# V of batches 2 and 3 issued by GpSimd, piece by piece, in place of SyncE

## The chip, the cores and the metric

The kernel runs on one core of one Trainium2 chip. The metric is device time in microseconds (us) of one execution. The engines of a core have short names in the profile: PE is TensorE (matmul), PEld its weight load, DVE is VectorE, ACT is ScalarE, POOL is GpSimd, SP is SyncE, which here only issues transfers. A transfer issued by POOL goes through one queue (q0, "software_dynamic"), one issued by SP through another (q1, "hardware_dynamic"); both are served by the same 16 DMA engines. Each engine works through its own instructions strictly in order, and waits on semaphores for the others.

## The reference

Eight batches of eight heads of causal attention with a learned decay, and behind them a gated feed-forward block. Shapes: q, k, v are 8 x 8 x 576 x 64, s is 8 x 8 x 576, the weights are 512 x 1536 (twice) and 1536 x 512, all float32.

```python
def _attn_ref(q, k, v, s):
    scores = scale * np.matmul(q, k.transpose(0, 1, 3, 2))
    causal = np.triu(np.ones((S, S), dtype=bool), k=1)
    cum = np.cumsum(np.maximum(s, 0.0), axis=-1)
    bias = -(cum[:, :, :, None] - cum[:, :, None, :])
    scores = np.where(causal, -1000000000.0, scores + np.minimum(bias, 0.0))
...
    return np.matmul(attn, v)

def _moe_ref(x, w_gate, w_val, w_out):
    g = x @ w_gate
    silu = g * (1.0 / (1.0 + np.exp(-g)))
    return (silu * (x @ w_val)) @ w_out
```

attn is the softmax of the scores, and x is the attention's output with the heads of a token side by side: 4608 tokens of 512.

## The kernel before, in words

**Units of work.** The attention goes head by head (64 of them, numbered 0 to 63, eight to a batch; the code calls the number `bh` or `kk`). Four heads are a head block (`hb`, or `h` in `side`, 16 of them; `HB = 4`, so two blocks to a batch); `step` is the head within its block. A head's scores are computed in four pieces, `ci` 0 to 3 (`score_piece`, L352): PE makes the products (L374), ACT the exponential into the tile `pt` (L384), and POOL puts zeros above the diagonal, for piece 0 at L387 and for piece 3, the tail of 64 columns, at L392. These two are "the masks". The product with V (`av_piece`, L409) comes one or more heads later, then DVE divides by the row sums (L425, L426).

**The feed-forward block** works on tiles of 512 tokens (`tt`). For each tile there are twelve gate blocks and twelve value blocks (L649, weights `wg` and `wv`), with ACT's tanh at L670 and DVE's products at L672 and L683, and then the product with w_out (L706 for the first two tiles, L755 for the later ones, which use a seven-product scheme). The weights are loaded by POOL, in halves or quarters (`w_load`, L346).

**How the two are woven.** PE's order is written out by hand. The head of the program (to about 40 us) computes the attention of batch 0 and begins the first token tile. Then a loop runs through the feed-forward items of each tile and, after each item, lets the generator `attn_items` go on to a position that grows with the items done (`pump`). After every score piece `attn_items` calls `side(h, step, ci)` and `side_v(h, step, ci)`, which issue what has its place there: loads, casts, copies. So a place such as (4, 2, 2) means: after score piece 2 of head 4 * 4 + 2 = 18. An entry such as (H + 4, 3), with H = 8, means: after score piece 3 of head 12. Some more loads are hung on items of the first tile (`at_item`).

**V.** `load_v` (L156) loads V of one batch in five pieces by token rows (four of 128 rows, 256 KB each, one of 64 rows), each one transfer, into the float32 tile `rawv`, of which there is one buffer. `cast_v` (L167) casts a piece to bfloat16 into `vt` (two buffers). V of batch 0 and 1 is loaded by POOL. V of batch 1 is cast by POOL at heads 11 and 12 (`V1_AT`). V of batch 2 is loaded by SP, with one call after score piece 3 of head 12 (L485), and cast by POOL at heads 17 and 18 (`V2_AT`, L540). V of batch 3 is loaded by SP, two pieces after head 18's piece 1 (L526), three after head 19's (L530), and cast by ACT at heads 21 to 23 (`V_AT`, L542, the cast itself is L171). V of batches 4 to 7 is loaded by SP and cast by ACT in the same way.

**K and Q.** `load_one` (L145) loads K or Q of one head block (576 KB) into one of three buffers each (`rawk`, `rawq`). Blocks 2 to 5 are loaded by POOL, blocks 6 and later by SP: block 6 after head 16's piece 1 (L487), block 7 after head 18's. They are cast to bfloat16 (`cast_one`, L258 on ACT, L260 on POOL). Up to block 4 PE transposes them (L301) and ACT or DVE copies them out (L328, L330). From block 5 on SP writes the cast to DRAM (`scratch`, L274), reads it back transposed (`transposes`, L284), and DVE copies the halves into the tile `kq` (`split`, L288). The rows of `kq` that carry the decay are copied from the tile `HL` by `aug` (L188), four small transfers for each block, issued by POOL from block 4 on.

**The rest of POOL's work** in the stretch of the change: the casts of K and Q of blocks 4 and 5, stores of finished outputs (L727), and from batch 2 on the writes of the attention's output to DRAM (`x_out`, L443), which SP reads back transposed (L450). Later POOL also makes subtractions for the feed-forward block (L692, L820).

Of the kernel before, what the change touches and what calls it, by code (L numbers as in the profile page):

```python
# [19 lines left out]
def kernel(  # L20
# [11 lines left out]
    nc = tc.nc  # L32
    PSUM = bass.MemoryType.PSUM

    B, H, S, D = q.shape
# [78 lines left out]
    with tc.manual_schedule():  # L114
# [26 lines left out]
        def load_one(hb, name, rs=(0, NR), eng=nc.sync):  # L141
            b, g = divmod(hb, 2)
            if rs[0] == 0:
                loaded[name, hb] = raw.tile([128, NR, J, D], FP32, tag="raw" + name, name="raw" + name)
            eng.dma_start(  # L145
                loaded[name, hb][:, rs[0] : rs[1], :, :].rearrange("x r j d -> x r (j d)"),
                SRC[name][0][b, g * HB + 2 * rs[0] : g * HB + 2 * rs[1], :, :].rearrange(
                    "(r e) (p j) d -> (e p) r (j d)", e=2, j=J
                ),
            )  # L150

        def load_qk(hb):
            load_one(hb, "k")
            load_one(hb, "q")

        def load_v(b, cs, eng=nc.sync):  # L156
            if 0 in cs:
                loaded["v", b] = raw.tile([128, NCH, H, D], FP32, tag="rawv", bufs=1, name="rawv")
            t = loaded["v", b]
            for c in cs:  # L160
                n = 128 if c < 4 else TAIL
                eng.dma_start(  # L162
                    t[0:n, c, :, :],
                    v[b, :, c * 128 : c * 128 + n, :].rearrange("h p d -> p h d"),
                )

        def cast_v(b, c, eng):  # L167
            n = 128 if c < 4 else TAIL
            dst, src_t = VT[b % 2][0:n, c, :, 0:D], loaded["v", b][0:n, c, :, :]
            if eng is nc.scalar:  # L170
                nc.scalar.copy(dst, src_t)  # L171
            else:
                eng.tensor_copy(dst, src_t)
# [9 lines left out]
        def aug(hb, engs, hhs=range(HB)):  # L183
            for hh in hhs:
                r, e = divmod(hh, 2)
                r0 = 64 * (1 - r)
                bh = hb * HB + hh
                engs[hh].dma_start(  # L188
                    KQ[hb % 2][r][r0 : r0 + 4, :, e * S : (e + 1) * S],
                    HL[bh : bh + 1, :, :, :],  # L190
                )
# [61 lines left out]
        def cast_one(hb, name, eng):  # L253
            cts[name, hb] = cp.tile([128, J, NR, D], BF16, tag="c" + name, bufs=2, name="c" + name)
            dst = cts[name, hb].rearrange("x j r d -> x r j d")
            src_t = loaded[name, hb]
            if eng is nc.scalar:
                nc.scalar.copy(dst, src_t)  # L258
            else:
                eng.tensor_copy(dst, src_t)  # L260
# [11 lines left out]
        def scratch(hb):  # L272
            for name, SC in (("k", KS), ("q", QS)):
                nc.sync.dma_start(  # L274
                    SC[hb].rearrange("(x j) c -> x (j c)", j=J),
                    cts[name, hb].rearrange("x j r d -> x (j r d)"),
                )
# [3 lines left out]
        def transposes(hb):  # L281
            for name, SC in (("k", KS), ("q", QS)):
                prs[name, hb] = cp.tile([128, NR * S], BF16, tag="p" + name, bufs=1, name="p" + name)
                nc.sync.dma_start_transpose(prs[name, hb], SC[hb])  # L284
# [185 lines left out]
        def do_later(n):  # L470
            while n > 0 and later:
                f, *args = later.pop(0)
                f(*args)
                n -= 1
# [2 lines left out]
            (H + 3, 3): (0, 1), (H + 4, 0): (2,), (H + 4, 1): (3,), (H + 4, 2): (4,)  # L477
        }

        def side(h, step, ci):  # L480
            bh = HB * h + step
            for c in V1_AT.get((bh, ci), ()):
                cast_v(1, c, nc.gpsimd)
            if bh == H + 4 and ci == 3:
                load_v(2, range(5))  # L485
            if h == 4 and (step, ci) in ((0, 1), (2, 1)):
                load_qk(6 + step // 2)  # L487
            if h >= 5 and h + 3 < NHB and (step, ci) == (0, 1):
                if h == 6:
                    load_one(h + 3, "k")  # L490
                else:
                    load_qk(h + 3)
            hb = h + 1
            if NPE <= hb < NHB:
                late = hb == NPE
                if late and (step, ci) == (0, 1):
                    scratch(hb)
                if late and (step, ci) == (0, 3):
                    transposes(hb)
                if (step, ci) == (0, 1):  # L500
                    aug(hb, GP4)
                first = 1 if hb < NPE + 3 else 0
                if step in (first, first + 1) and ci == (3 if late else 1):
                    for r in range(NR):
                        later.append((split, hb, "kq"[step - first], r))
            hb = h + 2
            if hb == NPE and step == 3 and ci % 2 == 1:
                cast_one(hb, "kq"[ci // 2], nc.gpsimd)
            if NPE < hb < NHB:
                six = hb == NPE + 1  # L510
                if (step, ci) == ((2, 0) if six else (0, 2)):
                    cast_one(hb, "k", nc.scalar)
                if (step, ci) == ((2, 2) if six else (1, 2)):
                    cast_one(hb, "q", nc.scalar)
                if (step, ci) == ((3, 0) if six else (2, 0)):
                    scratch(hb)
                if (step, ci) == (3, 3 if six else 0):
                    do_later(NR * 2)
                    transposes(hb)
            if ci != 1:  # L520
                return
            bn = h // 2 + 1
            if 3 <= bn < B:
                if h % 2 == 0:
                    if step == 2 and h != 6:
                        load_v(bn, (0, 1))  # L526
                    if step == 3:
                        if h == 6:
                            load_one(h + 3, "q")
                        load_v(bn, (2, 3, 4))  # L530
# [36 lines left out]
        def attn_items():  # L567
            for kk in range(H, BH + 2):
                h, step = divmod(kk, HB)
                if kk < BH:  # L570
                    if step == 0:
                        do_later(NR * 2)
                    if step == 1 and 3 < h + 1 < NPE:
                        cast_one(h + 1, "k", nc.gpsimd)
                        cast_one(h + 1, "q", nc.gpsimd)
                    if step == 2 and 3 < h + 1 < NPE:
                        aug(h + 1, GP4)
                    for ci in range(4):
                        score_piece(kk, ci)
                        side(h, step, ci)  # L580
                        side_v(h, step, ci)
                        yield kk + 0.1 + ci / 8
                        if (step, ci) in PREP_AT.get(h, ()):
                            prep_one(
                                h + 1, PREP_AT[h][step, ci],
                                (nc.scalar, nc.vector)[ci // 2] if h == 2 else None,
                            )
                            yield kk + 0.1 + ci / 8
# [327 lines left out]
        def pick(side):  # L916
            b = PICK[side]
            for lo in range(2):
                for c0, c1 in ((0, 512), (512, S)):
                    nc.tensor.matmul(  # L920
                        banks[:, b + c0 // 512, 0 : c1 - c0], sel[:, lo, :],
                        HL[:, lo, 1, c0:c1], start=(lo == 0), stop=(lo == 1),
                        skip_group_check=True,
                    )

        def picked_row(side):
            b = PICK[side]
            src_t = banks.rearrange("p b n -> p (b n)")[up, b * 512 : b * 512 + S]
            dst = KQ[0][0][up, side, 0:S]
            if side == 1:  # L930
                nc.scalar.activation(
                    dst, src_t, AF.Identity, bias=r_m[up, 0:1], scale=r_k[up, 0:1]
                )
            else:
                nc.vector.tensor_scalar(
                    dst, src_t, r_q[up, :], r_k[up, :], ALU.mult, ALU.add
                )
            give(b)
            give(b + 1)
# [195 lines left out]
```

## Time and profile before

| | |
|---|---|
| three runs, us | 372.74, 372.95, 375.08; median 372.95 |
| profiled execution, us | 372.82 (span of the profile 371.1) |
| granted TensorE clock | 1.0 |
| DMA, whole span | 64.21 MB, mean 173 GB/s |
| queue of SP (q1) | 79188 packets, 37.92 MB |
| queue of POOL (q0) | 13072 packets, 25.75 MB |
| V pieces issued by SP | 30, median 762 ns each (367 to 3786) |
| V pieces issued by POOL | 10, median 903 ns each (696 to 1322); 4.5 to 11.2 us from issue to landing, median 7.5 |

The whole span in 40 slices of 9.3 us each; a digit is the busy share in tenths:

```profile
PE   7899999999999999999999999999999999999995
DVE  8878786288985999589968987699768867975984
ACT  8979776778886976687858875786466423323321
POOL 8998785945366556694749465955575506315220
DMA  7999999999999975995699575996161113002003
```

A span is the time from the first to the last instruction of the profiled execution; the device time is a little longer. Times inside the profile are counted from the start of the span. In an order of time, a line gives start, length, engine, source line, operation, what is written and read, how many instructions were merged, and in brackets the idle time before and what ended it. A line of waits gives the engine and line that waited, for whom, the total, how many times, and the longest. "To landing" is the time from the issue of a transfer to its completion.

### The profile page before, as it was taken

How to read it: one execution, taken by the hardware profiler on the slowest of the kernel's cores; microseconds unless marked ns; L12 is line 12 of the kernel's file. 1: busy time of each engine (PE TensorE's matmuls, PEld its weight loads, DVE VectorE, ACT ScalarE, POOL GpSimd, SP SyncE). 2: the span in 40 equal slices, each digit the busy share in tenths (PEclk: the TensorE clock that was granted, in tenths of full speed). 3: DMA queues.
4: the chain of work that ended last, by engine and by line, in shares of the span. 5: the costliest groups of instructions: out<-in, count | busy, mean ns of one | idle time of the engine just before them, and what ended most of it. 6: DMA issues, size and time to landing. Idle time of an engine off the chain costs nothing.

```text
span 371.1 us, 8778 instructions
## 1 busy us (share of the span) xinstructions
PE 362.7 (98%) x3286; PEld 229.9 (62%) x3286; DVE 289.9 (78%) x583; ACT 241.2 (65%) x472; POOL 220.6 (59%) x336
## 2 busy tenths in 40 slices
PE   7899999999999999999999999999999999999995
PEld 6685566555555557755685568555865585476464
DVE  8878786288985999589968987699768867975984
ACT  8979776778886976687858875786466423323321
POOL 8998785945366556694749465955575506315220
PEclk9999999999999999999999999999999999999999
DMA  7999999999999975995699575996161113002003
GB/s 236 213 271 285 196 295 253 246 360 180 246 223 249 287 162 167 220 328 158 175 184 261 168 197 173 234 160 160 40 147 36 35 35 113 0 2 103 13 0 113
DMA packets 92301, 64.21 MB, mean 173 GB/s; under 512 B 72620, under 2 KB 78116, under 8 KB 92260
## 3 DMA queue, kind: packets, MB, share of 16 engines
q1 hardware_dynamic: 79188, 37.92, 44.1%
q0 software_dynamic: 13072, 25.75, 26.5%
q8 instruction: 25, 0.41, 0.5%
q14 instruction: 16, 0.13, 0.1%
HBM read 37.90 MB, written 19.86 MB: 156 GB/s over the span
## 4 chain that ended last, share of the span: by engine, by line
PE 88%; DVE 4%; POOL 4%; ACT 1%; issue 1%; DVEq 0%; POOLq 0%
PE banks L649 46%; PE banks L755 17%; PE banks L374 10%; PE banks L409 8%; PE banks L706 5%; DVE kq L330 2%; POOL rawv L162 1%; DVE pp L672 1%; DVE ht L683 1%; PE banks L301 1%; ACT pt L384 1%; PE banks L458 1%; DVE kq L288 0%; POOL ck L260 0%; POOL cq L260 0%
## 5 line engine op out<-in xcount | busy, mean ns | idle before, releaser
L384 ACT ACTIVATE pt<-banks 128x512 bf16<-128x512 f32 (+1 forms) x256 | 120.6, 511 | 28.2 <-PE banks L374 16.1
L649 PE MATMUL banks<-XT,wg 128*128 128x512 bf16 x432 | 111.4, 380 | 0.0
L649 PE MATMUL banks<-XT,wv 128*128 128x512 bf16 x432 | 110.9, 379 | 0.1
L670 ACT ACTIVATE th<-banks 128x512 bf16<-128x512 f32 x108 | 64.7, 599 | 54.8 <-PE banks L649 49.5
L672 DVE SCALAR_TENSOR_TENSOR pp<-th,banks 128x512 bf16<-128x512 bf16 x108 | 73.7, 682 | 19.4 <-ACT th L670 18.8
L683 DVE SCALAR_TENSOR_TENSOR ht<-pp,banks 128x512 bf16<-128x512 bf16 x108 | 74.1, 686 | 10.6 <-DVE pp L672 0.5
L374 PE MATMUL banks<-kq 128*128 128x128 bf16 (+4 forms) x576 | 76.3, 240 | 0.4 <-DVE kq L288 0.3
L692 POOL TENSOR_TENSOR ht<-ht 128x512 bf16<-128x512 bf16 x35 | 40.4, 1154 | 53.0 <-DVE su L690 52.9
L374 PEld LDWEIGHTS <-kq 128*128 128x128 bf16 x576 | 45.9, 98 | 29.8 <-issue 1.7
L649 PEld LDWEIGHTS <-wv 128*128 128x128 bf16 x432 | 38.4, 98 | 36.1 <-issue 0.2
L649 PEld LDWEIGHTS <-wg 128*128 128x128 bf16 x432 | 38.3, 98 | 33.6
L387 POOL TENSOR_SCALAR_AFFINE_SELECT pt<-pt 128x512 bf16<-128x512 bf16 x58 | 38.2, 658 | 24.8 <-ACT pt L384 22.7
L409 PEld LDWEIGHTS <-pt 128*128 128x128 bf16 x960 | 41.9, 98 | 17.4 <-issue 0.2
L409 PE MATMUL banks<-vt,pt 128*128 128x65 bf16 x960 | 46.8, 194 | 0.0
L443 POOL DMA_DIRECT2D xs<-ot x24 | 21.7, 903 | 29.3 <-DVE ot L426 28.7
L755 PEld LDWEIGHTS <-ht 128*128 128x128 bf16 x336 | 31.2, 98 | 4.3
L426 DVE TENSOR_TENSOR ot<-banks,rc 128x320 bf16<-128x320 f32 x64 | 31.5, 492 | 2.2
L188 POOL DMA_DIRECT2D kq<-HL x48 | 28.9, 604 | 0.5 <-issue 0.4
L706 PE MATMUL banks<-wo,ht 128*128 128x512 bf16 x96 | 25.8, 380 | 0.0
L755 PEld LDWEIGHTS <-su 128*128 128x128 bf16 x252 | 23.5, 98 | 3.3
L820 POOL TENSOR_TENSOR ysb<-ysb 128x512 f32<-128x512 f32 x12 | 15.2, 1270 | 15.3 <-DVE ysb L814 15.3
L755 PE MATMUL banks<-WS,ht 128*128 128x256 bf16 x168 | 22.9, 273 | 0.0
(101 smaller groups left out, 383.9 us busy)
## 6 DMA issues: line engine op xcount, KB each, us to landing
out_dram<-ysb POOLq DMA_DIRECT2D x32, 256.0 KB, 4.0
rawv<-in_v_dram SPq DMA_DIRECT2D x24, 256.0 KB
rawk<-in_k_dram SPq DMA_DIRECT2D x10, 576.0 KB
rawq<-in_q_dram SPq DMA_DIRECT2D x10, 576.0 KB
xs<-ot POOLq DMA_DIRECT2D x24, 160.0 KB, 3.5
ks<-ck SPq DMA_DIRECT2D x11, 288.0 KB
qs<-cq SPq DMA_DIRECT2D x11, 288.0 KB
rawk<-in_k_dram POOLq DMA_DIRECT2D x5, 576.0 KB, 7.5
```

The costliest lines, as they stand in the source:

```text
L374: nc.tensor.matmul(sc[:, o : o + w], T[:, 1, e * S + 128 * tj : e * S + 128 * (tj + 1)], T[:, 0, e * S + lo : e * S + hi], start=not maske ...
L384: nc.scalar.activation(pt[:, c0 : c0 + n], sc, AF.Exp, scale=0.125)
L387: nc.gpsimd.affine_select(pt[:, 1088:1600], pt[:, 1088:1600], pattern=[[0, 4], [1, 128]], compare_op=ALU.is_ge, fill=zreg, base=0, channel ...
L409: nc.tensor.matmul(av[:, bi * (D + 1) : (bi + 1) * (D + 1)], pt[:, c0 : c0 + 128], VT[b % 2][:, tj, h, :], start=(tj == 0), stop=(tj == bi),)
L426: nc.vector.tensor_mul(ot[:, :, e * D : (e + 1) * D], av3[:, :, 0:D], rc[:, :, None].to_broadcast([128, NCH, D]),)
L649: nc.tensor.matmul(view(bs, TT), w[:, c, f0 : f0 + 128], xt[:, c, :], start=(c == 0), stop=(c == 3),)
L670: nc.scalar.activation(th, pg, AF.Tanh, scale=0.5)
L672: nc.vector.scalar_tensor_tensor(pp, in0=th, scalar=1.0, in1=pg, op0=ALU.add, op1=ALU.mult)
L683: nc.vector.scalar_tensor_tensor(hp[:, 2 * k2 : 2 * k2 + 2, :].rearrange("p a n -> p (a n)"), in0=pp, scalar=0.5, in1=pv, op0=ALU.mult, op ...
L692: (nc.vector if ft == NFT - 1 else nc.gpsimd).tensor_sub(hp[:, 1:3, :], hp[:, 1:4:2, :], hp[:, 0:3:2, :])
L706: nc.tensor.matmul(view(pys[ts_], DM), hps[ft // 2][:, 2 * (ft % 2) + half, c0 : c0 + 128], WO[j][:, ft % WKO, :], start=(ft == 0), stop=( ...
L755: nc.tensor.matmul(ps, lhs(p), rhs(p), start=(first and p == 0), stop=(last and p == NP - 1), skip_group_check=True,)
```

## The change

The five pieces of V of batch 2 are no longer issued by SP in one call after head 12, but by POOL, one piece each after heads 12 (piece 3), 13 (pieces 1 and 3) and 14 (pieces 1 and 3). V of batch 3 is no longer issued by SP after heads 18 and 19, but by POOL, one piece each after head 18 (score piece 2), head 19 (pieces 0 and 2) and head 20 (pieces 0 and 2). The old calls are taken out: the condition `3 <= bn` becomes `3 < bn`, so that SP's calls remain for batch 4 and later. Within a place, the V load comes ahead of what `side` and `side_v` issue there after it.

```diff
+        V2_LOAD = {
+            (H + 4, 3): (0,), (H + 5, 1): (1,), (H + 5, 3): (2,), (H + 6, 1): (3,),
+            (H + 6, 3): (4,),
+        }
+        V3_LOAD = {
+            (4, 2, 2): (0,), (4, 3, 0): (1,), (4, 3, 2): (2,), (5, 0, 0): (3,), (5, 0, 2): (4,)
+        }
+
         def side(h, step, ci):
             bh = HB * h + step
             for c in V1_AT.get((bh, ci), ()):
                 cast_v(1, c, nc.gpsimd)
-            if bh == H + 4 and ci == 3:
-                load_v(2, range(5))
+            for c in V2_LOAD.get((bh, ci), ()):
+                load_v(2, (c,), nc.gpsimd)
+            for c in V3_LOAD.get((h, step, ci), ()):
+                load_v(3, (c,), nc.gpsimd)
             if h == 4 and (step, ci) in ((0, 1), (2, 1)):
                 load_qk(6 + step // 2)
...
             bn = h // 2 + 1
-            if 3 <= bn < B:
+            if 3 < bn < B:
                 if h % 2 == 0:
                     if step == 2 and h != 6:
                         load_v(bn, (0, 1))
```

## The prediction

> **What bounds the kernel now.** I read the page's first lines, then busy time by stage, then the longest waits of SP's queue, then the orders of time of SP, POOL, PE and DVE around the moved loads, and for single transfers the time from issue to landing.
>
> ```profile
> span 371.1 us, 8778 instructions
> PE 362.7 (98%) x3286; PEld 229.9 (62%) x3286; DVE 289.9 (78%) x583; ACT 241.2 (65%) x472; POOL 220.6 (59%) x336
> ```
>
> TensorE is the bound: it is idle for 8.4 us in all. The stages say where (columns: stage, length, busy time of PE, PEld, DVE, ACT, POOL, granted clock, DMA share, GB/s).
>
> ```profile
> 50.00:55.00 5.00, 5.00 (x67) 3.36 (x64) 4.11 (x9) 3.12 (x7) 4.99 (x8) 1.00 1.20 253
> 55.00:60.00 5.00, 5.00 (x71) 3.45 (x69) 3.44 (x8) 3.73 (x9) 3.66 (x8) 1.00 1.13 313
> 60.00:65.00 5.00, 5.00 (x70) 3.34 (x68) 3.56 (x8) 3.17 (x6) 1.88 (x4) 1.00 0.85 209
> ...
> 80.00:85.00 5.00, 4.75 (x42) 2.68 (x41) 4.87 (x11) 3.25 (x7) 3.26 (x6) 1.00 1.20 315
> ```
>
> V of batch 2 is loaded at 51 to 62 us, V of batch 3 at 76 to 83. In all of 40 to 100 us PE misses 0.26 us, at 82.42, before the scores of head 20, where it waits for a copy on DVE (L288). Nothing there waits for V. So the change has 0.26 us to win in its own stretch, and every new wait of PE is paid in full, for PE has no later gap to take it back.
>
> Next SP: its longest waits (us in total, times, longest), then its order of time (start, length).
>
> ```profile
> SPq L162 <- DMA rawv<-in_v_dram: 19.2, 2, 18.6
> SPq L162 <- POOL vt L173: 10.9, 2, 8.2
> ...
> 21.05 2.25 SPq L188 DMA_DIRECT2D kq<-HL  x2
> 50.98 10.69 SPq L162 DMA_DIRECT2D rawv<-in_v_dram  x5
> 61.71 0.62 SPq L145 DMA_DIRECT2D rawk<-in_k_dram  x1
> ```
>
> SP stands at the V load from 23.3 to 51.0: 18.6 us until V of batch 1 has landed, 8.2 more until POOL has cast it (there is one V buffer). Then it takes 10.7 us to issue five pieces. Behind them in SP's order is the load of K and Q of head block 6, at 61.71.
>
> **The change part by part.** *Removed from SP:* 10.69 us of issue, and 0.99 + 3.34 us for batch 3 at 75.97 and 79.71. By itself it gains nothing on PE; it shortens SP's road to the transposes of block 6, whose results DVE takes only at 90.7. I count 0.
>
> *Moved by it: K and Q of block 6.* Their three-deep buffers were last used by block 3, and POOL's casts of that block end at 36.88 + 1.16 = 38.04 (K) and 37.96 + 1.16 = 39.12 (Q). With the V load gone, nothing else holds SP, so these 1,152 KB are issued 23 us earlier. They meet these loads, which POOL put on its own queue and PE will want (last column: us to landing); below them, in order of time, who takes them:
>
> ```profile
> wv<-in_moe_w_val_dram POOLq DMA_DIRECT2D x1, 384.0 KB, 9.7
> rawk<-in_k_dram POOLq DMA_DIRECT2D x1, 576.0 KB, 10.5
> ...
> 47.91 1.03 PE L649 MATMUL banks<-XT,wv 128*128 128x512 bf16 x4
> 51.82 1.15 POOL L260 CAST ck<-rawk 128x1152 bf16<-128x1152 f32 x1
> 54.38 0.44 PE L301 MATMUL banks<-ident,ck 128*128 128x128 bf16 x5
> ```
>
> The last quarter of the value weights is issued at 36.11 and lands at 45.8; the tenth value block needs it at 47.91: 2.1 us of room. K of block 4, issued at 40.68, lands at 51.2 and is cast at 51.82. The 16 DMA engines are full there (share 1.1 to 1.3 in every stage from 24 to 60 us), so bytes put in push back what stands behind. How far: where the same two loads now run almost alone, at 64 to 68 us, the stage shows 386 GB/s, so 1.18 MB hold the engines for 3.1 us. Lower end 0 (they fit beside), upper end 6 us (the 190 GB/s of the full stages). I take 3.0, by the row of the very same loads. The weights then land at 48.8, and PE waits 48.8 - 47.91 = 0.9 us. K of block 4 lands at 54.2, is cast by about 55.35, and PE, already 0.9 late, wants it at 54.38 + 0.9 = 55.3: no second wait to speak of. **+0.9 us** (0 to 3.9, the end at 6 us of delay). The Trainium skill (DMA: Bandwidth & Descriptors, Queues, rings and completion order) says that each DMA engine goes round-robin between the queues that have work, a packet at a time, which is why a load from SP would not queue up behind POOL's. With that page's HBM limit of 358 GB/s the estimate would be 3.3 us of delay, a wait of 1.2, and 374.5 for the sum below.
>
> *Added to POOL: ten issues.* POOL's own V issues of batches 0 and 1 took 903 ns (median; 696 to 1322): 4.5 us for each batch (3.5 to 6.6). POOL's idle time is 0.01 + 1.34 + 3.12 = 4.5 us in 50 to 65, and 3.34 + 1.74 + 2.92 = 8.0 in 75 to 90, so both batches fit; what counts is what stands behind each piece in POOL's order. For batch 2: the casts of K and Q of block 4 (priced above), the masks of heads 13 to 15, and four small bias copies for block 4 (L188). They were issued from 56.01 on and the first landed 5.9 us later, at 61.9; the scores of head 16 need it at 65.69. With three pieces ahead (2.7 us) and casts that wait for late K and Q (1.5), the first goes out near 59.9 and lands at 65.8; PE wants it at 66.6. Cost 0, with 0.8 us to spare. The mask of head 14's tail, 59.90, moves to about 64 and is read near 66.5. The pieces need no new wait: POOL itself made the casts that free the buffer. Their data: V pieces from POOL landed in 7.5 us (at most 11.2), and the last one, issued near 64.5, is cast at 75.32.
>
> For batch 3 I follow POOL again, then DVE and PE (start, length; idle before in brackets):
>
> ```profile
> 77.91 0.23 POOL L392 TENSOR_SCALAR_AFFINE_SELECT pt<-pt 128x64 bf16<-128x64 bf16 x1 [1.48 <-ACT pt L384]
> 81.11 0.91 POOL L443 DMA_DIRECT2D xs<-ot  x1 [2.97 <-DVE ot L426]
> ...
> 76.52 0.45 DVE L288 COPY kq<-pk 64x1152 bf16<-64x1152 bf16 x1
> 81.33 0.95 DVE L288 COPY kq<-pq 64x1152 bf16<-64x1152 bf16 x1
> 82.42 0.38 PE L374 MATMUL banks<-kq 128*128 128x128 bf16 x4 [0.26 <-DVE kq L288]
> ```
>
> The first piece fits the 1.48 us gap at 76.43. Four more, 3.6 us, fall between 82.65 and 89.5; the mask of head 20's tail moves from 86.85 to about 89.5 and is read near 90.6. Cost 0, with 1 us to spare (with 1.32 us for each piece it would be 0.6 late). The casts of V on ACT, at 87.98 to 98.75, come 4 us or more behind the landings that 7.5 us would give for the first pieces, 2 us for the last.
>
> But the first piece lies upon the L288 copy at 76.52, and DVE works without a break from 75.12 to the copy that PE waits for. The same copy takes 0.45 us with POOL still and 0.95 at 81.33, with POOL issuing L443; at 142.29, under L188 issues, it took 0.45. So 0 to 0.9 us; I take the middle, which is also what the L443 row adds (0.95 - 0.45, less a little), an issue of 0.91 us like a V piece's: **+0.45 us**, and PE's wait at 82.42 grows from 0.26 to 0.7. The Trainium skill (SBUF — State Buffer, SBUF: two separate sides) has VectorE's two-port modes and GpSimd share a port pair as an exclusive lock, and its rules for kernel authors advise against issuing from GpSimd under such a copy. By a full lock the copy would wait out the whole 0.9 us issue, and the sum would be 374.6; the 0.45 at 142.29 speaks against a lock at every issue.
>
> **Sum.** The profiled execution took 372.82 us (span 371.1 and 1.72 around it), 0.13 below the median of the runs, 372.95. 372.82 + 0.9 + 0.45 = 374.2. That is the forecast.
>
> **Rivals.**
> *Nothing is late: not slower.* SP does run ahead, but the early K and Q delay the weights by less than their 2.1 us of room, and the copy at 76.52 keeps its 0.45 us. For it: the second half of w_out, issued at 45.58 with V of batch 2 coming in beside it, took 11.1 us to land, and the first half, issued at 39.25 with nothing beside it, 10.4; so a second queue need not cost its whole time. Against: the DMA share over 1, and V of batch 2 came in small packets, 10.7 us long, where K and Q come at once. Time 372.6 (the 0.26 us goes as well) to 373.1. It is also what comes of it if SP is held by something I don't see and issues block 6 no earlier, so that the change does not do what its order says. 30%.
> *The early loads hold POOL's queue back twice as long: slower by over 1%.* At the 190 GB/s end the delay is 6 us. The weights land at 51.8 and PE stands 3.9 us; K of block 4 lands at 57.2, is cast by 58.4, and PE, by then 3.9 late, comes for it at 58.3, so that wait isn't paid again; POOL's pieces and bias copies, behind the late casts, move by no more than PE. 372.82 + 3.9 + 0.45 = 377.2. It decides where the delay passes 5.4 us (5.4 - 2.1 + 0.45 = 3.7). For it: the full stages do move only that much. Against: they move small pieces, and the two loads' own row says half of it. 9%.
> *Faster by over 1%,* 369.2 or less: it needs 3.7 us, and PE's idle time lies before 40 us and in the last stage, which the change does not reach. 1%.
> *My forecast,* a loss of 0.3 to 3.7 us: 60%.
>
> **How the numbers follow.** 1%, 3.7 us, is about what a measurement of this kernel can tell from no change. The forecast and the first rival lie within it: 90%; slower 9%; faster 1%. The range goes from 372.6, the floor of the first rival, to 376.3, which is 372.82 + 3.0 + 0.45, a delay of 5.1 us at the weights: it leaves out the 9% above it and what little lies under the floor.
>
> **What would show it.** K and Q of block 6 issued by SP at 38 to 40 us, not 61.7; the weights' landing at 48 to 49 and a wait of PE before its tenth value block; POOL's V issues near 0.9 us each; the copy at 76.5 near 0.9, and PE's wait for L288 near 0.7. I am wrong if SP issues block 6 where it did, if PE's stages from 40 to 60 stay full, or if a new wait appears at L409 (a mask) or at L374 of head 16 (the bias copies).

## The result, and the profile after

The changed kernel takes 375.56 us (median; 374.02 to 378.6 over 20 runs), the kernel before on the same chip 373.11 (372.7 to 377.15): a ratio of 1.0054, with a 95% interval of 1.0035 to 1.0072, so about 2 us, or 1.3 to 2.7, slower. That lies within 1%. A ratio here is worked out from the fast runs alone (a run over 1.5% above its kernel's fastest counts as slow: two of twelve with both loads held, one of twelve with block 6 held) and need not be the quotient of the two medians beside it. The profiled execution of the changed kernel took 376.83 us (span 375.0), over its median; so I also read a second one, of 374.41 us (span 372.6), and call a loss this change's own only where both have it.

The first lines of the changed kernel's page:

```profile
span 375.0 us, 8780 instructions
PE 364.2 (97%) x3286; PEld 230.3 (61%) x3286; DVE 289.5 (77%) x583; ACT 241.4 (64%) x472; POOL 228.8 (61%) x346
```

TensorE does the same 3,286 matmuls and stands 10.8 us of the span in place of 8.4. POOL is busy for 8.2 us more. Busy time by stage shows where PE stands (columns as in the prediction):

```profile
45.00:50.00 5.00, 4.40 (x29) 2.10 (x28) 4.12 (x6) 3.99 (x8) 4.14 (x8) 1.00 1.19 263
60.00:65.00 5.00, 5.00 (x66) 3.44 (x65) 3.56 (x8) 3.39 (x8) 4.99 (x9) 1.00 0.84 235
95.00:100.00 5.00, 5.00 (x54) 2.91 (x51) 4.71 (x10) 4.61 (x11) 1.46 (x3) 1.00 0.41 107
110.00:120.00 10.00, 9.50 (x82) 5.25 (x81) 4.96 (x11) 6.08 (x13) 4.81 (x9) 1.00 1.07 243
120.00:135.00 15.00, 14.61 (x124) 7.99 (x122) 12.91 (x26) 12.09 (x24) 8.44 (x13) 1.00 1.16 252
```

and two of these stages in the kernel before:

```profile
95.00:100.00 5.00, 5.00 (x49) 2.86 (x47) 4.74 (x10) 4.07 (x10) 2.01 (x4) 1.00 0.94 226
110.00:120.00 10.00, 10.00 (x90) 5.67 (x89) 5.05 (x12) 6.24 (x14) 6.43 (x12) 1.00 0.90 229
```

PE misses 0.6 us at 45 to 50, 0.5 at 110 to 120 and 0.39 at 120 to 135; before, these stages were full (4.99, 10.00 and 15.00). POOL is busy throughout 60 to 65, where it was for 1.88 us, and no PE time is lost there. At 95 to 100 the DMA engines run at a share of 0.41 and 107 GB/s; before, at 0.94 and 226. That hole is the first sign of something the prediction did not have.

The order of time of SP, of the changed kernel:

```profile
38.29 0.40 SPq L145 DMA_DIRECT2D rawk<-in_k_dram  x1
39.38 0.39 SPq L145 DMA_DIRECT2D rawq<-in_q_dram  x1
...
88.97 0.53 SPq L145 DMA_DIRECT2D rawk<-in_k_dram  x1
89.59 0.41 SPq L145 DMA_DIRECT2D rawq<-in_q_dram  x1
97.64 3.38 SPq L450 DMA_TRANSPOSE XT<-xs  x2
...
111.31 2.40 SPq L450 DMA_TRANSPOSE XT<-xs  x2
```

and the same stretch of the kernel before:

```profile
90.18 0.89 SPq L145 DMA_DIRECT2D rawk<-in_k_dram  x1
91.20 0.41 SPq L145 DMA_DIRECT2D rawq<-in_q_dram  x1
92.69 2.74 SPq L450 DMA_TRANSPOSE XT<-xs  x2
...
108.64 2.42 SPq L450 DMA_TRANSPOSE XT<-xs  x2
```

K and Q of block 6 go out at 38.29 and 39.38, as forecast. But SP is also ahead fifty microseconds later: K of block 8 goes out at 88.97, not 90.18. The next item in SP's order is a transposed read (L450) of the attention output of head pair 9, which POOL has to write to DRAM first. That read starts at 97.64, not 92.69, and the last of its kind ahead of the third token tile of the feed-forward block (`tt` = 2) at 111.31, not 108.64. SP's longest wait at 84 to 125 us in the changed kernel is the one for pair 9's write (us in total, times, longest); the kernel before stood 1.0 us for the same write:

```profile
SPq L450 <- DMA xs<-ot: 7.6, 1, 7.6
```

Single transfers of the changed kernel, from issue to landing (last column, us): the last quarter of the value weights, and pair 9's write.

```profile
wv<-in_moe_w_val_dram POOLq DMA_DIRECT2D x1, 384.0 KB, 12.5
...
xs<-ot POOLq DMA_DIRECT2D x1, 160.0 KB, 6.8
```

Pair 9's write in the kernel before:

```profile
xs<-ot POOLq DMA_DIRECT2D x1, 160.0 KB, 3.0
```

The weights took 9.7 us before. The delay of the weights, 2.8 us, is the one forecast (3.0); w_out's first half, K of block 4 and Q of block 4 were 2.8, 2.7 and 2.9 late. The Trainium skill (DMA: Bandwidth & Descriptors, Queues, rings and completion order) has each DMA engine alternate between queues, and the trace agrees: a load from SP moved four POOL loads by one like amount, the weights among them, which had gone out 2 us ahead of it (36.34 and 38.29). The Trainium skill's 358 GB/s (Specifications of the same page) gave an estimate of 3.3 us; the rows are nearer to the 3.1 us that follow from the 386 GB/s of the same loads' own stage.

PE's waits from 45 to 135 us in this execution (idle time before, in brackets):

```profile
48.90 1.04 PE L659 MATMUL banks<-XT,wv 128*128 128x512 bf16 x4 [0.59 <-DMA wv<-in_moe_w_val_dram]
83.49 0.38 PE L374 MATMUL banks<-kq 128*128 128x128 bf16 x4 [0.25 <-DVE kq L288]
117.86 0.38 PE L659 MATMUL banks<-XT,wg 128*128 128x512 bf16 x1 [0.50 <-DMA XT<-xs]
131.15 1.02 PE L659 MATMUL banks<-XT,wg 128*128 128x512 bf16 x4 [0.17 <-DVE ht L693]
132.39 0.46 PE L409 MATMUL banks<-vt,pt 128*128 128x65 bf16 x10 [0.22 <-DVE ot L426]
```

The first is the forecast wait for the weights. The second, at L288's copy, has not grown. The third waits for the transposed reads that SP made late. The last two come from Q of block 9, which SP also loaded later (122.78 for 117.13): ACT stands 0.83 us for it before its cast at 127.82, and then DVE and PE are late.

How late PE is at each point can be worked out by taking the same matmul of both traces, start after less start before; what is added at a place is that place's price:

| place | first execution | second execution |
|---|---|---|
| by 25 us, ahead of anything edited | +0.23 | +0.09 |
| weights, 48.9 | +0.75 | +0.70 |
| 50 to 55.5, with K of block 4 | +0.08 | +0.01 |
| L288's copy, 83.5 | 0 | 0 |
| transposed reads, 117.9 | +0.66 | +0.34 |
| Q of block 9, 131 to 132 | +0.71 | +0.66 |
| 191 | -0.17 | -0.17 |
| K of a later block, 247 to 251 | +1.75 | 0 |

Without the first row and the last, the change costs 2.0 us in one execution and 1.5 in the other; the ratio says 1.3 to 2.7. In the runs below PE is up to 2.7 us late by 22 us, in kernels that are all the same up to there, so the first row is not counted to the change.

### The profile page after: what moved, and what is told of

The parts are those of the page before. It is cut to its first block, busy times and chain, and to the rows that moved or that the text cites. A ratio compares the mean times of both kernels' runs of the same rounds, so it can differ in the third digit from the quotient of the medians.

```text
span 375.0 us, 8780 instructions
## 1 busy us (share of the span) xinstructions
PE 364.2 (97%) x3286; PEld 230.3 (61%) x3286; DVE 289.5 (77%) x583; ACT 241.4 (64%) x472; POOL 228.8 (61%) x346
## 4 chain that ended last, share of the span: by engine, by line
PE 77%; DMA 10%; DVE 5%; POOL 3%; ACT 2%; issue 1%; SPq 1%; DVEq 0%; ACTq 0%; POOLq 0%
PE banks L659 41%; PE banks L765 17%; PE banks L374 8%; PE banks L409 6%; PE banks L716 4%; DMA wv<-in_moe_w_val_dram 3%; DMA pk<-ks 2%; DMA rawv<-in_v_dram 2%; DMA XT<-xs 2%; DVE pp L682 1%; DMA rawk<-in_k_dram 1%; DVE ht L693 1%; DVE kq L288 1%; ACT pt L384 1%; DVE kq L330 1%
## 5 line engine op out<-in xcount | busy, mean ns | idle before, releaser
L374 PE MATMUL banks<-kq 128*128 128x128 bf16 (+4 forms) x576 | 76.3, 240 | 1.2 <-DVE pp L682 0.5
L374 PEld LDWEIGHTS <-kq 128*128 128x128 bf16 x576 | 45.9, 98 | 30.7 <-issue 2.0
L409 PEld LDWEIGHTS <-pt 128*128 128x128 bf16 x960 | 41.8, 98 | 19.2 <-issue 2.2
L409 PE MATMUL banks<-vt,pt 128*128 128x65 bf16 x960 | 46.7, 194 | 0.8 <-DVE ot L426 0.7
L443 POOL DMA_DIRECT2D xs<-ot x24 | 22.0, 915 | 26.8 <-DVE ot L426 26.2
L188 POOL DMA_DIRECT2D kq<-HL x48 | 29.1, 608 | 0.1
```

The lines of the kernel that those rows point to most:

```text
L374: nc.tensor.matmul(sc[:, o : o + w], T[:, 1, e * S + 128 * tj : e * S + 128 * (tj + 1)], T[:, 0, e * S + lo : e * S + hi], start=not maske ...
L409: nc.tensor.matmul(av[:, bi * (D + 1) : (bi + 1) * (D + 1)], pt[:, c0 : c0 + 128], VT[b % 2][:, tj, h, :], start=(tj == 0), stop=(tj == bi),)
```

## The experiments

Several theories stood against each other; the letters are those of the expectations. A: K and Q of block 6, early, hold back the weights (A as first written also had V of batch 3 hold back pair 9's write; C had the second loss follow from the first). B: POOL's issues cost POOL or DVE time that PE pays. D: SP runs ahead, loads block 8 ahead of pair 9's write, and then stands for that write, in order, with everything behind it late. E: what holds back that write are the V pieces ahead of it in POOL's own queue. Each kernel ran in five rounds beside the kernel before, whose medians in the three sets were 373.14, 373.6 and 373.52 us. "Late" is PE's lateness as in the table above. HOLD and HOLD8 below are DRAM tiles of 128 bytes that nothing reads: SP writes them from a tile that has to be ready first, so that it stands until then.

**One batch alone.** Batch 3's loop is taken out and SP's calls put back; then the same for batch 2.

```diff
-            for c in V3_LOAD.get((h, step, ci), ()):
-                load_v(3, (c,), nc.gpsimd)
...
-            if 3 < bn < B:
+            if 3 <= bn < B:
```

```diff
-            for c in V2_LOAD.get((bh, ci), ()):
-                load_v(2, (c,), nc.gpsimd)
+            if bh == H + 4 and ci == 3:
+                load_v(2, range(5))
```

> Only V of batch 2 goes to POOL; V of batch 3 stays on SP. Theory A (two separate losses: K and Q of block 6, issued early by the freed SP, push back the last value weights; V of batch 3 in POOL's queue pushes back the attention writes that SP waits for): PE waits about 0.6 us for the value weights near 48.9 us, their landing takes 12 to 13 us instead of 9.7, and there is no wait for XT at 117 us. Time 0.7 to 1.2 us over before. Rival B (the issues on POOL, in order ahead of its masks, cost the time): PE waits at a mask, half of the whole loss, 1.2 us, for half of the issues.

> Only V of batch 3 goes to POOL; V of batch 2 stays on SP, so K and Q of block 6 are issued at 61 to 62 us as before. Theory A: no wait for the value weights; the attention write of pair 9, issued near 90 us, lands in 6 to 7 us instead of 3.0; SP's transposed read behind it goes out near 96 instead of 92.7, and PE waits for XT at tile 2 or for the copies of transposed K later on. Time 1 to 2 us over before. Rival C (the second loss is only what the first one pushed along): without the early loads there is no wait for XT and the time is that of before within 0.3 us.

Batch 2 alone: 376.35 us, 1.0074 [1.0047, 1.0101]. Batch 3 alone: 376.12, 1.0078 [1.0047, 1.0109]. Both are misses: 0.7 to 1.2 and 1 to 2 us over before had been expected, and the medians are 3.2 and 3.0 over. The halves do not add up: each costs as much as the whole or more. Their traces part the terms nonetheless. Batch 2 alone has the wait for the weights (0.38 us, late by 0.55, and 0.26 more by K of block 4), pair 9's write in 4.7 us and no loss at the transposed reads. Batch 3 alone has the weights in time, that write in 6.7 us and 0.82 lost at the reads. So the early block 6 comes from batch 2's edit, and most of SP's lead at 90 us from batch 3's. Both have two steps more, which the whole change lacks: 1.3 us at 140 (0.99 and 0.31 just behind it), and 0.34 and 0.95 us at 310. They are taken up below.

**Block 6 early, without any move to POOL,** in the kernel before, twice:

```diff
-            if bh == H + 4 and ci == 3:
-                load_v(2, range(5))
             if h == 4 and (step, ci) in ((0, 1), (2, 1)):
                 load_qk(6 + step // 2)
+                if step == 0:
+                    load_v(2, range(5))
```

> All V stays on SP as before; only the load of K and Q of block 6 is put ahead of V of batch 2 in SP's order. Theory A: they are issued at 38 to 39 us, the value weights land in 12 to 13 us and PE waits 0.6 us for them; 0.6 to 1.0 us over before, with nothing moved to POOL. Rival B: no loss, since POOL has no new issues.

> All V on SP, only K and Q of block 6 ahead of V of batch 2, once more: in its first profile PE was already 2.1 us late at 22 us, ahead of anything that was edited, and so could not show a wait for the value weights. Theory A: the weights land in 12 to 13 us, and where PE is not late from the start it waits about 0.6 us for them; 0.5 to 1.5 us over before.

374.61, 1.0018 [0.9991, 1.0045], and 374.25, 1.0010 [0.9989, 1.0030]: not to be told from the kernel before. In the first profile block 6 went out at 40.07 and the weights landed in 9.1 us; PE was already 2.0 us late by 22 us there, so the profile decides nothing. In the second block 6 went out at 38.84 and the weights took 11.8 us, but PE, here 0.8 us late by 22 us, lost only 0.05 for them; it lost 0.36 at K of block 4 and 0.49 at 131:

```profile
55.52 0.45 PE L301 MATMUL banks<-ident,ck 128*128 128x128 bf16 x5 [0.20 <-POOL ck L260]
```

So block 6 issued early delays the weights and K of block 4 without one V issue on POOL, but alone it costs less than five rounds can tell.

**Block 6 held back, the change kept.** SP stands for a tile written at 60 to 61 us:

```diff
+            if (h, step, ci) == (3, 3, 0):
+                nc.sync.dma_start(HOLD, XT[0:1, 1, S : S + D])
             if h == 4 and (step, ci) in ((0, 1), (2, 1)):
                 load_qk(6 + step // 2)
```

> The change as it is, and on SP, ahead of K and Q of block 6, one transfer of 128 bytes that reads what DVE writes at 60 to 61 us, so that SP stands there as before. Theory A: K and Q of block 6 are issued near 61 us, the value weights land in 9.7 us, PE's wait for them is gone, and 0.8 us of the change's 2.45 come back; the wait for XT may stay. Rival B: no change against the changed kernel.

Block 6 went out at 61.48, the weights landed in 9.9 us and PE did not wait for them: that term is gone with its cause. The time was 374.57, 1.0010 [0.9978, 1.0043]; level with before as far as this tells, and not clear of the changed kernel either. But theory D's wait was there, and larger (1.92 us lost), as pair 9's write took 8.9 us:

```profile
118.28 0.38 PE L662 MATMUL banks<-XT,wg 128*128 128x512 bf16 x1 [1.76 <-DMA XT<-xs]
```

**Block 8 behind the read of pair 9,** in the changed kernel (e6); **block 8 sooner,** in the kernel before (e9), where its load goes ahead of the transposed read that it followed:

```diff
-            if h >= 5 and h + 3 < NHB and (step, ci) == (0, 1):
+            if h >= 5 and h + 3 < NHB and (step, ci) == ((2, 0) if h == 5 else (0, 1)):
```

```diff
-            if h >= 5 and h + 3 < NHB and (step, ci) == (0, 1):
+            if h >= 6 and h + 3 < NHB and (step, ci) == (0, 1):
...
                     transposes(hb)
+                    if six:
+                        load_qk(8)
```

> The changed kernel, with the load of K and Q of block 8 moved behind the transposed read of pair 9 in SP's order. In the profiles so far the landing of pair 9's attention write goes with the head start that this load has over it: load 0.5 us behind the write, 3.0 us to land; level with it, about 4.8; 0.3 ahead, 5.8; 1.8 ahead, 6.8. Theory D (the load of block 8, let go earlier by the freed SP, gets its 1.18 MB in front of the write): the write lands in 3 to 4 us, SP's read of it goes out near 94 instead of 97.6, no wait for XT at tile 2; 0.5 to 1.5 us less than the changed kernel, with the wait of 0.6 us for the value weights still there. Theory E (the V pieces ahead of the write in POOL's own queue): it still lands in 6 to 7 us and the time stays.

> The kernel before, with all V on SP, and only the load of K and Q of block 8 put ahead of the transposed read of pair 8 in SP's order, so that it goes out near 88 us, about 2 us ahead of pair 9's write instead of 0.5 behind it. Theory D: that write lands in 6 to 7 us, the read behind it goes out near 96.5 instead of 92.7, and the kernel before loses 1 to 3 us without any V moved. Theory E: the write lands in 3 to 4 us and nothing is lost.

Behind the read, the write landed in 3.6 us and the read of pair 9 went out at 94.72. Theory D's landing holds; E's does not, for the V pieces still stood ahead of the write (the last at 90.16, the write at 91.14). The time did not come back, a miss: 376.23, 1.0090 [1.0053, 1.0126], over 8 runs. SP's order of time says why:

```profile
94.72 2.39 SPq L450 DMA_TRANSPOSE XT<-xs  x2
97.17 0.57 SPq L145 DMA_DIRECT2D rawk<-in_k_dram  x1
97.79 0.46 SPq L145 DMA_DIRECT2D rawq<-in_q_dram  x1
98.35 0.41 SPq L274 DMA_DIRECT2D ks<-ck  x1
98.86 0.38 SPq L274 DMA_DIRECT2D qs<-cq  x1
104.40 1.22 SPq L284 DMA_TRANSPOSE pk<-ks  x1
...
113.27 3.63 SPq L450 DMA_TRANSPOSE XT<-xs  x2
```

The load, at 97, now stands ahead of block 7's scratch writes; SP waits 5.1 us for the first of them, and the last read is later still. PE waits 1.10 us for it. The delay was moved, not removed. In the kernel before, the lead was made as large as in the changed kernel (89.52 against 91.17): the write took 5.6 us, near what D says (6 to 7), but the time was 373.99, 1.0012 [0.9992, 1.0031], with no wait of PE at 118, where a loss of 1 to 3 us had been expected. PE was 1.5 us late by 22 us in this profile, which may have hidden a wait. A slow write alone did not cost time here; how late SP is at the last read is compared below.

**The change once more, unedited; and both edits at once** (block 6 held as above, block 8 behind the read of pair 9 as in e6):

> The changed kernel once more, unedited, beside the others on the same chip and for a second profile. The waits that belong to the change should come again: about 0.6 us for the value weights near 48.9, about 0.5 for XT near 118. The waits of its first profile at 131 and 247 us, through DVE, may be one execution's own: if so they are absent or elsewhere. Median 375 to 376.

> All V of batches 2 and 3 on POOL as in the change, with both loads held back: block 6 by the 128-byte transfer that waits for DVE at 60 to 61 us, block 8 behind the transposed read of pair 9. If the early loads are the whole loss (theory D with the first finding), this is level with the kernel before, within 0.5 us, with the ten issues on POOL still there; if the issues or POOL's queue cost anything of themselves, that rest is left: 1 us or more.

The change again: 374.91, 1.0042 [1.0023, 1.0062]; its profile is the second column of the table. PE's waits in it for the weights and for the reads:

```profile
48.70 1.04 PE L659 MATMUL banks<-XT,wv 128*128 128x512 bf16 x4 [0.54 <-DMA wv<-in_moe_w_val_dram]
...
117.29 0.38 PE L659 MATMUL banks<-XT,wg 128*128 128x512 bf16 x1 [0.18 <-DMA XT<-xs]
```

Both edits at once: 378.61 us, 1.0163 [1.0118, 1.0208], over 6 runs. It had been expected level with before, a plain miss. The profiled execution is its longest (383.73 us). Block 8 went out only at 101.67, the last read at 119.15, and PE stood 4.8 us for it; behind that the granted clock was 0.50 from 124 to 128 us, and PE lost 2.5 us more before it was at 1.00 again. The place of a load in an in-order queue can be wrong on both sides.

**Each half with its early load held,** and **the whole change with both held.** Batch 2 alone gets the hold of block 6 shown above; block 8 is held by pair 9's own data, so that it can't pass the write:

```diff
+            if (h, step, ci) == (5, 1, 0):
+                nc.sync.dma_start(HOLD8, kept[9][0:1, 0, D : 2 * D])
+                load_qk(8)
-            if h >= 5 and h + 3 < NHB and (step, ci) == (0, 1):
+            if h >= 6 and h + 3 < NHB and (step, ci) == (0, 1):
```

(`kept` holds the tiles of attention output that `x_out` sends.)

> V of batch 2 alone on POOL, and K and Q of block 6 held on SP by a 128-byte transfer that waits for DVE at 60 to 61 us. If the early load is the whole cost of that half (theory A), the value weights land in under 10 us, no wait for them, XT's last read goes out near 108.6 plus what PE is late, and the time is that of before within 0.5 us. If POOL's five issues or their data cost something of themselves, 1 us or more stays.

> V of batch 3 alone on POOL, and K and Q of block 8 held on SP by a 128-byte transfer that reads what DVE writes just before pair 9's attention write goes out, so that they follow that write by about half a microsecond, as in the kernel before, and are no later than there. Theory D (their head start over the write is what matters): the write lands in 3 to 4 us instead of 6.7, XT's last read goes out near 109 instead of 111, no wait for XT, and the time is that of before within 0.5 us. Theory E (V pieces ahead in POOL's queue): the write still lands in 6 us or more, and 1 us or more stays.

> The whole change with both loads held as in the two runs beside it. Theories A and D together: level with the kernel before, within 0.5 us, and 1.5 us or more under the changed kernel. If something else of the change costs time, the time stays above 374.5.

Batch 2 with block 6 held: 375.22, 1.0046 [1.0018, 1.0074]. The weights landed in 9.0 us, pair 9's write in 2.8, the last read went out at 108.53, where it was before, and PE was not late at all until 139 us. Batch 3 with block 8 held: 376.44, 1.0073 [1.0043, 1.0104]. Here the hold came out shorter than meant: block 8 went out 0.09 us behind pair 9's write, not half a microsecond, and the write took 5.6 us, not 3 to 4. Still the last read went out at 109.41 in place of 110.99, and the 0.82 us that PE lost at the reads without the hold is gone; PE falls no further behind until 139. Both times miss the level of before that had been expected, by 1.7 and 2.9 us. In both profiles the loss begins at 139, with the first of the two steps that the plain halves had too. Both profiled executions are the shortest of their twelve (374.55 and 374.58), so what the medians have above them, 0.7 and 1.9 us, is in no trace. The orders of time of POOL, DVE and PE for batch 2 with block 6 held:

```profile
135.44 0.89 POOL L444 DMA_DIRECT2D xs<-ot  x1 [2.54 <-DVE pp L683]
136.34 0.66 POOL L388 TENSOR_SCALAR_AFFINE_SELECT pt<-pt 128x512 bf16<-128x512 bf16 x1
136.98 1.14 POOL L703 TENSOR_TENSOR ht<-ht 128x512 bf16<-128x512 bf16 x1
...
136.44 1.84 DVE L702 TENSOR_TENSOR su<-ht 128x256 bf16<-128x256 bf16 x1
...
138.93 0.38 PE L375 MATMUL banks<-kq 128*128 128x320 bf16 x2 [0.83 <-DVE pp L683]
```

and of the kernel before:

```profile
134.45 0.89 POOL L443 DMA_DIRECT2D xs<-ot  x1 [1.45 <-DVE ot L426]
135.36 0.65 POOL L387 TENSOR_SCALAR_AFFINE_SELECT pt<-pt 128x512 bf16<-128x512 bf16 x1
136.70 1.15 POOL L692 TENSOR_TENSOR ht<-ht 128x512 bf16<-128x512 bf16 x1 [0.69 <-DVE su L690]
...
136.53 0.28 DVE L691 TENSOR_TENSOR su<-ht 128x256 bf16<-128x256 bf16 x1
```

POOL stands 2.54 us before one issue in place of 1.45. Its mask and its subtraction are then done in one run, from 136.34 to 138.12, and DVE's small sum, which ran in 0.28 us in the gap between them, starts at 136.44, inside that run, and ends at 138.28, after it: 1.84 us. PE loses 1.00 us here and 0.32 more at 141. The Trainium skill (SBUF — State Buffer, SBUF: two separate sides) has a VectorE operation with two SBUF inputs and a GpSimd operation that reads SBUF shut each other out for the whole instruction; these rows agree, and here the sum waited out two such operations. All four kernels with five V issues more on POOL show the 2.53 to 2.54 us; kernels with none more or with ten more show 1.44 or 1.45. The same four are late at one more POOL issue, the last write of attention output: it goes out 1.83 us after DVE has written its tile and in the other kernels 0.30 us after (303.96 with block 6 held, 301.13 before). PE then loses 0.3 to 1.0 us at 308 to 311, waiting for a transposed read. Why these issues are late by their number is open. The first of them waits for one semaphore of DVE in all kernels; in the four it goes out 0.17 us after DVE's next product, pp, so a wait for a later instruction of DVE is not ruled out. So the halves are no fair price list of the whole.

The whole change with both loads held: 374.24, 0.9990 [0.9956, 1.0024], level with before, as expected, though 0.7 and 1.3 us under the two medians of the change, not 1.5 or more. Block 6 went out at 62.40, the weights landed in 8.8 us, and PE did not wait for them. The profiled execution is one of its longer ones (375.47 us), PE being 1.1 late from the start, and in it pair 9's write took 7.5 us although block 8 went out behind it (0.74 us):

```profile
118.50 0.38 PE L667 MATMUL banks<-XT,wg 128*128 128x512 bf16 x1 [1.05 <-DMA XT<-xs]
```

In that execution PE lost 1.21 us at the reads and 0.64 at Q of block 9: what the change loses by SP's lateness is there in full. So by the medians the loss is gone as far as five rounds tell, and V on POOL as such gains nothing and costs at most what the interval leaves, 0.0024 of 373.52 or 0.9 us. The trace shows only the wait for the weights gone. What the hold of block 8 adds to that of block 6 (374.57 by itself) is not shown, and why the shorter executions are shorter is not in a trace. The interval lies below that of the change's first measurement (1.0035 to 1.0072) and just touches the second (1.0023 to 1.0062). No version here beats the kernel before.

**Across the runs.** Two relations can be checked on all profiles. The wait at 118 follows SP's lateness: the issue of the last read less PE's lateness at that time, and what PE lost there, are

| kernel | last read, us | PE lost, us |
|---|---|---|
| before; batch 2, block 6 held; block 6 early (second) | 108.6; 108.6; 108.9 | 0; 0; 0 |
| batch 3, block 8 held; batch 2 alone | 109.2; 109.3 | 0; 0 |
| block 8 sooner; block 6 early (first) | 110.0; 110.2 | 0; 0 |
| the change (first, second) | 110.2; 110.3 | 0.66; 0.34 |
| batch 3 alone; block 8 later | 111.1; 111.8 | 0.82; 1.26 |
| both held; block 6 held | 112.1; 112.3 | 1.21; 1.92 |
| block 6 held, block 8 later | 116.5 | 5.3, and 2.5 at the lower clock |

The edge is near 110.2. The two kernels just at it without a loss are those whose PE was 1.5 and 2.0 us late from the start.

What makes pair 9's write slow is less clear. Where block 8's load was issued from 0.1 us behind it to 1.9 ahead of it, it took 4.5 to 8.9 us; with the load 0.5 behind, in the kernel before, 3.0; with the load well behind, 2.8 and 3.6. But with both held it took 7.5, and with block 6 held and block 8 eight microseconds later 6.0. In these two block 7's transposed reads went out only at 84.6 and 85.8 us (80.7 in the changed kernel), and V pieces were in flight; neither was varied by itself. That block 8's load delays the write is shown for the changed kernel by moving that load; that nothing else does so is not. And that this load's place is what makes PE wait at 118 is shown in a trace for batch 3 alone, where holding it took the wait away; for the whole change no run took that wait away, and the chain from the load to the wait is read from the traces.

## Why the prediction was right, and where it was not

The direction and the size class came out: 374.2 forecast, 375.56 measured, in the range and within 1%, by a sum of which one term held, one was empty and one was missing. That the number comes so near is in part luck: the empty 0.45 stood where 1.0 to 1.4 was missing.

*K and Q of block 6, +0.9 us: right, step by step.* Issued at 38.29 and 39.38; the weights landed at 48.84 (forecast 48.8), PE waited 0.59 us and lost 0.7 to 0.8 with K of block 4. The wait is gone wherever block 6 is held back. The rival "nothing is late" falls by the 12.5 us of that landing, the rival of twice the delay by the same row.

*The copy at L288, +0.45 us: wrong, it is 0.* It is now at 77.60, starting with a V issue of 0.93 us, and takes 0.45 as before; at 83.97, under two more (83.79 to 85.79), 0.46. DVE's order of time, changed kernel:

```profile
77.60 0.45 DVE L288 COPY kq<-pk 64x1152 bf16<-64x1152 bf16 x1
82.40 0.94 DVE L288 COPY kq<-pq 64x1152 bf16<-64x1152 bf16 x1
83.97 0.46 DVE L288 COPY kq<-pq 64x1152 bf16<-64x1152 bf16 x1
91.77 0.91 DVE L288 COPY kq<-pk 64x1152 bf16<-64x1152 bf16 x1
```

I took the price from L443's issue, as the row of like length. The slow copies start 0.21 us into such an issue of attention output (82.40) or within a mask (91.77). The row that should have served was the one I had against it, the 0.45 under L188's issues at 142.29. The rule of the Trainium skill that I weighed there, by which an issue would block the copy for its whole length, does not show at any V issue in this trace.

*POOL's issues in POOL's gaps, 0: right for the whole change,* though not for the halves, where two later POOL issues are late. The issues took 0.72 to 1.12 us each, the first bias copy of block 4 went out at 59.99 (forecast 59.9), the mask of head 20's tail at 90.52 (89.5), and no wait appeared at L409 for a mask or at L374 of head 16.

*"Removed from SP ... By itself it gains nothing on PE; it shortens SP's road to the transposes of block 6 ... I count 0": the step that failed.* I followed what SP's freedom does at 38 us and not what it does at 85 to 90, where the same order of work puts block 8's load ahead of a write it had followed. Of the 1.5 to 2.0 us of recurring loss, 1.0 to 1.4 (the reads at 118 and Q of block 9) comes from what SP issued late; how much of that lateness is block 8's load alone stays open. Two loads were let go early; the prediction followed one of them to what it meets.

## What to carry to other kernels

Taking work off an in-order issuing queue does not only free time; it lets every later item of that queue go sooner, until the next thing that it waits for. Follow each of those items to the transfers that it will now meet, at all later places and not only the next, and to what stands behind it in the same order. If a wait that is removed had been spacing loads, a tiny transfer that reads a tile of the right moment can give the spacing back, as it did for block 6 (no wait for the weights); its moment has to be checked, for block 8 it came out 0.09 and 0.74 us behind the write and the write stayed slow.

## What the runs showed of the hardware that I had not expected

- A 160 KB write from POOL's queue took 3.0 us before, 6.8 us with K and Q of a block (1,152 KB) let go from SP 1.8 us ahead of it, and 3.6 with that load put behind its read. In one run it took 7.5 with the load 0.74 behind it, and why is open.
- A V issue on POOL did not slow DVE's copy (0.45 us); a mask did, and so did an issue of attention output begun 0.21 us before (0.91 and 0.94).
- DVE's sum of two SBUF tiles of 128x256 took 0.28 us in a gap between POOL's operations and 1.84 when it started inside two of them back to back.
- In the four kernels with five V issues more on POOL, two later POOL issues were 1.1 and 1.5 us late; with ten more they were not. The cause is open.
- After PE had stood 4.8 us, in one execution, the granted clock was 0.50 from 124 to 128 us.
- PE was up to 2.7 us late within the first 22 us of an execution, in kernels that differ from the one before only behind that point.
